# A recurrence that feeds a feed-forward network: a reordered opening before the first dense matmul

## The chip, the cores and the metric

The kernel runs on one core of a Trainium2 chip. The metric is the device time of one execution in microseconds (us), lower is better. A core has five engines with queues of their own: TensorE (PE, with weight loads listed as PEld), VectorE (DVE), ScalarE (ACT), GpSimd (POOL) and SyncE (SP). SP, ACT and POOL also issue the DMA transfers; an issue occupies the queue it stands in. Each engine works through its own list in order, and waits where an instruction needs something of another engine.

## The reference, cut to what matters

All inputs are 32-bit floats.

```python
# q, k, v: (4, 8, 768, 48)   beta: (4, 8, 768)
k_n = k / (norm(k) + 1e-6)
state = zeros(4, 8, 48, 48)
for t in range(768):
    y[:, :, t] = q[:, :, t] @ state
    v_old = state^T k_n[t]
    state = state + beta[t] * outer(k_n[t], v[t] - v_old)
x = y.transpose(0, 2, 1, 3).reshape(3072, 384)
# w1, w2, w3: (384, 768)   w_out: (768, 384)
h = maximum(maximum(x @ w1, x @ w2), x @ w3)
out = h @ w_out                       # (3072, 384)
```

## The kernel before, in words

The 768 steps are cut into 12 chunks of 64 steps. In a chunk, the products of its keys with each other (`gram`, tiles `at`) and of its queries with its keys (tiles `pt`) are made on PE. The chunk's recurrence becomes a triangular system. It is solved once for all batches and heads as blocks of 32 by 32 on DVE (`solve`: for each column one product into `tmp`, L617, and one subtraction from `y_bl`, L621). Two chunks make a pair `m`, and `solve(m)` serves both.

The first pair is different, and it is what the change is about. Its diagonal blocks of 32 are solved only as two halves of 16 (`HB`), so `solve(0)` has 15 columns instead of 31. PE then joins the halves in four matmul steps, each followed by copies out of PSUM: `halves_z` (p_e, L740, into `z`), `halves_u` (p_f, L751, negated back into `ut`), `join_z` (p_z, L768, into `z`) and `join_u` (p_j, L781, negated into `ut`). After these, `ut` holds the chunk's inverse. `new` (p_u, L826) multiplies it with the scaled values, `to_y` (p_y, L868) makes the outputs, and `to_x` (p_x, L887) transposes them into `xt`, the input of the network. For chunk 0 these steps work on two groups of four heads, so that one group's copy runs beside the other's matmuls.

What stands between the solution and `halves_u` is this. `solve(0)` ends with two transposes of 128x512 (L634) that turn the solution `y` back into `x_bl`; `placed` (L557) copies pieces of it into `ut`, on DVE, ACT and POOL; `halves_t` transposes `ut` into the tiles `t` (L700, L702), the stationary side of p_f.

The network (`ffn`) then runs in 6 groups of 512 tokens. `ffn(0)` is a generator of PE units of three matmuls of 256 columns (p_h, L1303). A table of the kernel (`FIRST`, `LINKS`, `CONVERTED` and others) says what is put into the queues after each unit: the rest of the recurrence, the steps of `solve(1)`, and the conversion of weights. In `ffn(0)` the steps of chunk 1 stand between the units: p_e, then p_s (L849, the update of the state, added by DVE at L856), p_f, then p_k (L798, the keys times the new state), and so on.

The weights arrive as 64-bit words in 24 pieces. `fetch` requests a piece into one of 5 buffers `w_bits`; `weights` makes three ACT passes on it (L255, L256, L257), `joined` makes a shift on DVE (L266) and an addition on POOL (L270) that writes `w_sb`. The join of one piece is made when the next is converted (`join_last`).

The order of all queues is written out by hand; no scheduler changes it. The opening is the straight list of calls in L1382 to L1464. Tiles are recycled: PSUM has three buffers of the tag `two`, so the fourth allocation waits for the copy out of the first.

Of the kernel before, what the change touches and what calls it, by code (L numbers as in the profile page):

```python
# [18 lines left out]
BL = 32  # L19
# [4 lines left out]
def kernel(  # L24
# [205 lines left out]
    waiting = []  # L230

    def join_last():
        if waiting:
            joined(*waiting.pop())

    def weights():
# [3 lines left out]
        for n, (dst, _, (a, b)) in enumerate(pieces):  # L240
            if n == 3 * FT:
                join_last()
                yield
            bits = staged.popleft().rearrange("p (a b two) -> p a b two", a=a, two=2)
            low, high = bits[:, :, :, 0], bits[:, :, :, 1]
            mant = work.tile([128, 384], U32, name="mant", bufs=2)
            up = work.tile([128, 384], I32, name="up", bufs=2)
# [7 lines left out]
            nc.scalar.mul(mant_v.bitcast(FP32), high.bitcast(FP32), 2.0**-112)  # L255
            nc.scalar.mul(halves[0], low, 2.0**-29)  # L256
            nc.scalar.mul(halves[1], high.bitcast(FP32), 2.0**-64)  # L257
            join_last()
# [299 lines left out]

    def solve(m):
# [27 lines left out]
        if m < 3:  # L587
            norm(k_bl, nt, root)
# [10 lines left out]
        nc.vector.tensor_tensor(out=xb, in0=xb, in1=by, op=ALU.mult)  # L599
        yield  # L600
# [26 lines left out]
        if m == 0:  # L627
            bl_0.append(k_bl)
            back, ahead = in_rows(xs[0]), y.rearrange("p c i -> p i c")
            A, V, P = nc.scalar.copy, nc.vector.tensor_copy, nc.gpsimd.tensor_copy  # L630
            for part, copies in (
                (slice(HB, BL), (P, A, P, A)), (slice(0, HB), (V, P, V, A)),
            ):
                nc.vector.transpose(out=back[:, part], in_=ahead[:, part])  # L634
                for i, copy in enumerate(copies):
                    placed(0, i, copy, part)
            yield
            return
# [65 lines left out]
    def heads_of(c, name, w):  # L704


        copies = (nc.scalar.copy,) if c else (nc.scalar.copy, nc.vector.tensor_copy)
        n = H // len(copies)
        for i, copy in enumerate(copies):
            p_v = ps_two(name)[:, :, 0 : n * w]  # L710
# [5 lines left out]
    def negated_of(c, name, w):  # L716
        if c:
# [3 lines left out]
        p = [  # L721
            ps_two(name)[:, :, 0 : NP * w].rearrange("p g (h x) -> p g h x", x=w)
            for _ in range(3)
        ]
        yield range(NP), (p[0], p[0]), (nc.scalar.mul,) * 2
        yield range(NP, H), (p[1], p[2]), (nc.scalar.mul, nc.vector.tensor_scalar_mul)
# [4 lines left out]
    def halves_z(c):  # L731
# [4 lines left out]
        for hs, p_v, copy in heads_of(c, "p_e", BL):  # L736
# [24 lines left out]
    def join_z(c):  # L761
        at = [ats.pop(2 * c + g) for g in range(2)]
        z, second = zs[c % NU], ut[c % NU][:, :, :, BL:C]
        for hs, p_v, _ in heads_of(c, "p_z", BL):
            for i, h in enumerate(hs):
                for bb, g in TILES:
                    r = block(bb, 1)
                    nc.tensor.matmul(  # L768
                        p_v[block(bb ^ g), g, i], at[g][r, h, 0:BL], second[r, g, h]
                    )  # L770
            for bb in range(2):
                nc.scalar.copy(z[block(bb), :, span(hs)], p_v[block(bb)])
# [101 lines left out]
    def to_x(c):  # L874
# [8 lines left out]
        for g in range(2):  # L883
# [9 lines left out]
            if not c:  # L893
                nc.scalar.copy(xt[:, g], of[:, g])  # L894
# [489 lines left out]
    load_beta_0()  # L1384
    load_k(6)
    load_q(0)
    load_k(7)
    load_q(1)
    fetch(nc.sync)
    busy(6, ident)  # L1390
# [15 lines left out]
    load_q(2, (nc.gpsimd, nc.gpsimd))  # L1406
    turn(4, (0,))
    turn(5, (0,))
    some(solving, 1)
    keys(4)  # L1410
    keys(5)
    turn(6, (0,))
    turn(0, (1,))
    load_q(3, (nc.gpsimd, nc.gpsimd))
    load_v(0)
    for _ in range(2):
        fetch(nc.sync)
    load_beta()
    keys(6)
    gram(0, (1,), None, later=True)()  # L1420
    turn(7, (0,))
    turn(1, (1,))
    keys(7)
    turn(2, (1,))
    gram(1, (1,), None, later=True)()
    some(conv, 1)
    turn(3, (1,))
    scores = [gram(n, (1,), None, later=True) for n in (2, 3)]
    some(solving, HB + 1)
    for copied in scores:  # L1430
        copied()
    halves_t(0)
    halves_z(0)
    first_norms()
    some(conv, 1)
    placed(1, 0)
# [214 lines left out]
```

## Time and profile before

Three timed executions took 501.72, 502.57 and 502.66 us; the median is 502.57 us. The profiled execution took 501.92 us, of which the span from first to last instruction is 500.0 us, so 1.92 us lie around it.

| | |
|---|---|
| PE busy | 480.2 us (96%) |
| DVE busy | 348.8 us (70%) |
| ACT busy | 169.6 us (34%) |
| POOL busy | 196.1 us (39%) |
| first matmul of the network (p_h) | at 44.06 us |
| chain that ended last | PE 88%, DVE 3%, DMA 2%, ACT 2%, "issue" 2% |
| mean granted TensorE clock | 0.976 |

How to read it: times are counted from the start of the span. A line of the timeline is a run of like instructions: start, length, engine, source line, operation, output and input, shapes, count, and in brackets the idle time before it with what ended it. "issue" is time in which an engine waited for nothing that the profile shows. A table by stretches gives, for each stretch, its length and then the busy time and the number of instructions of PE, PEld, DVE, ACT and POOL, then the granted clock, the share of the DMA engines, and GB/s. A 32-bit matmul stands as two PE and two PEld instructions, a transpose as one and one.

### The profile page before, as it was taken

The page shows a single profiled execution, that of the slowest core. Times are in us where ns is not written, and L with a number is a line of the kernel's source. Part 1 is how long each engine was busy: PE and PEld are TensorE (multiplying, and loading weights), DVE is VectorE, ACT ScalarE, POOL GpSimd, SP SyncE. Part 2 cuts the span into 40 slices and gives each one's busy share as a digit, 9 for nine tenths or more (in the row PEclk, how much of TensorE's full clock was granted, in tenths as well). Part 3 has the DMA queues.
Part 4 walks back from the last instruction along what each step waited for, and adds up shares of the span by engine and source line. Part 5 has one row for each costly group of instructions (what it writes and reads, how often), then busy time and mean ns, then how long its engine had stood idle before and what let it go on. Part 6 is the DMA issues. An engine that isn't in the chain of part 4 may idle for free.

```text
span 500.0 us, 18781 instructions
## 1 busy us (share of the span) xinstructions
PE 480.2 (96%) x8100; PEld 343.4 (69%) x8100; DVE 348.8 (70%) x819; ACT 169.6 (34%) x329; POOL 196.1 (39%) x330
## 2 busy tenths in 40 slices
PE   7869799999999999999999999999999999999997
PEld 6658688878665556565555565565797457988896
DVE  4888898656697352979552998565998864468753
ACT  5686665985330153201243200252211032212310
POOL 6557684764670394780575870601000020000000
PEclk9767899999999999999999999999999999999999
DMA  8948979874351655543775552833223330330001
GB/s 107 168 100 220 211 178 137 199 218 77 81 144 34 140 117 121 138 126 88 155 129 120 146 135 65 176 50 93 65 68 79 61 72 19 86 77 15 1 16 49
DMA packets 110114, 53.51 MB, mean 107 GB/s; under 512 B 93264, under 2 KB 103920, under 8 KB 110032
## 3 DMA queue, kind: packets, MB, share of 16 engines
q1 hardware_dynamic: 98528, 32.01, 31.8%
q0 software_dynamic: 9088, 19.72, 15.8%
q8 instruction: 64, 1.05, 0.9%
q10 hardware_dynamic: 2416, 0.59, 0.7%
q14 instruction: 18, 0.15, 0.1%
HBM read 39.17 MB, written 13.11 MB: 105 GB/s over the span
## 4 chain that ended last, share of the span: by engine, by line
PE 88%; DVE 3%; DMA 2%; ACT 2%; issue 2%; POOL 1%; SPq 1%; DVEq 0%; POOLq 0%; ACTq 0%
PE p_h L1303 34%; PE p_o L1346 13%; PE p_o L1040 10%; PE p_g L443 5%; PE p_c L1241 4%; PE p_u L826 3%; PE p_y L868 3%; PE p_k L798 2%; PE p_m L960 2%; PE p_t L366 2%; PE p_q L798 2%; PE p_s L849 2%; PE p_j L781 2%; PE p_z L768 2%; PE p_e L1241 1%
## 5 line engine op out<-in xcount | busy, mean ns | idle before, releaser
L1303 PE MATMUL p_h<-xt,w_sb 128*128 128x512 f32 (+1 forms) x468 | 177.7, 523 | 0.6 <-ACT xt L894 0.3
L1303 PEld LDWEIGHTS p_h<-xt,w_sb 128*128 128x128 f32 x468 | 85.1, 191 | 62.0 <-issue 53.0
L1317 DVE TENSOR_TENSOR h<-h,p_h 128x512 f32<-128x512 f32 (+1 forms) x42 | 23.9, 569 | 55.9 <-PE p_h L1303 53.4
L617 DVE TENSOR_TENSOR tmp<-x_bl,y_bl 128x31 f32<-128x31 f32 (+20 forms) x139 | 50.3, 362 | 4.0
L621 DVE TENSOR_TENSOR y_bl<-y_bl,tmp 128x31 f32<-128x31 f32 (+20 forms) x139 | 46.5, 334 | 4.8
L1346 PE MATMUL p_o<-wo_sb,h 128*128 128x384 f32 x144 | 49.2, 490 | 0.4 <-POOL wo_sb L270 0.4
L1313 ACT ACTIVATE h<-p_h 128x512 f32<-128x512 f32 (+1 forms) x30 | 16.6, 552 | 76.2 <-PE p_h L1303 76.2
L401 POOL DMA_DIRECT2D turned<-in_q_dram x72 | 39.2, 552 | 5.1 <-POOL turned L396 2.6
L1346 PEld LDWEIGHTS p_o<-wo_sb,h 128*128 128x128 f32 x144 | 26.8, 190 | 18.5 <-POOL wo_sb L270 1.0
L443 PEld LDWEIGHTS p_g<-kqt 48*64 48x64 f32 x1184 | 23.5, 138 | 11.5 <-issue 7.1
L443 PE MATMUL p_g<-kqt 48*64 48x64 f32 (+1 forms) x1184 | 26.7, 238 | 2.9 <-ACT kqt L372 2.9
L270 POOL TENSOR_TENSOR w_sb<-mant,up 128x384 int32<-128x384 int32 x18 | 18.5, 1032 | 23.7 <-DVE mant L266 20.0
L1352 ACT COPY o_sb<-p_o 128x384 f32<-128x384 f32 x12 | 5.7, 478 | 61.7 <-PE p_o L1346 41.7
L396 POOL MEMSET turned<- 128x96 f32 x18 | 3.3, 190 | 59.1 <-DVE kqt L417 59.1
L653 POOL DMA_DIRECT2D ut<-y_d x4 | 2.6, 651 | 60.4 <-DMA y_d<-y_bl 60.4
L148 POOL DMA_DIRECT2D v_t<-in_v_dram x14 | 11.6, 830 | 28.7 <-PE p_u L826 28.7
L856 DVE TENSOR_TENSOR st<-st,p_s 48x768 f32<-48x768 f32 (+1 forms) x18 | 17.1, 951 | 7.7 <-PE p_s L849 7.3
L810 DVE TENSOR_TENSOR v_t<-v_t,p_k 128x768 f32<-128x768 f32 x11 | 10.4, 949 | 15.3 <-PE p_k L798 15.3
L1346 PE MATMUL p_o<-w_sb,xt 128*128 128x384 f32 x60 | 21.0, 486 | 0.0
L427 DVE TENSOR_TENSOR pt<-p_g,mask 128x512 f32<-128x512 f32 x20 | 13.7, 689 | 10.4 <-PE p_g L443 10.3
L460 ACT COPY at<-p_g 128x512 f32<-128x512 f32 x22 | 12.7, 583 | 18.8 <-DVE pt L427 16.5
L401 POOL DMA_DIRECT2D turned<-in_k_dram x32 | 17.5, 553 | 3.0 <-DMA v_t<-in_v_dram 1.9
(252 smaller groups left out, 917.4 us busy)
## 6 DMA issues: line engine op xcount, KB each, us to landing
w_bits<-in_moe_w_dram SPq DMA_DIRECT2D x9, 384.0 KB, 5.3
w_bits<-in_moe_w_dram POOLq DMA_DIRECT2D x9, 384.0 KB, 4.8
turned<-in_q_dram POOLq DMA_DIRECT2D x72, 48.0 KB, 2.6
out_dram<-o_sb SPq DMA_DIRECT2D x34, 96.0 KB, 2.3
y_x<-y SPq DMA_DIRECT2D x32, 96.0 KB, 2.3
qall<-y_x SPq DMA_DIRECT2D x32, 96.0 KB, 2.9
v_t<-in_v_dram POOLq DMA_DIRECT2D x14, 192.0 KB, 4.5
at_d<-at SPq DMA_DIRECT2D x76, 32.0 KB, 2.9
```

The costliest lines, as they stand in the source:

```text
L270: nc.gpsimd.tensor_tensor(out=dst.bitcast(I32), in0=mant_v.bitcast(I32), in1=up_v, op=ALU.add)
L401: (queue, nc.gpsimd)[i].dma_start(out=t[p0 : p0 + 32, bb, at : at + NP * 2 * D].rearrange("p (j x) -> p j x", j=NP), in_=(k, q)[i][2 * bb ...
L443: nc.tensor.matmul(p_g[rows(bb ^ (g * i)), par, c0 : c0 + C * (1 + whole)], kq[:, 0], kq if whole else kq[:, i],)
L617: nc.vector.tensor_tensor(out=t_v, in0=row.to_broadcast(t_v.shape), in1=column.to_broadcast(t_v.shape), op=ALU.mult,)
L621: nc.vector.tensor_tensor(out=rest, in0=rest, in1=t_v, op=ALU.subtract)
L798: nc.tensor.matmul(p_b[rows(bb), par, c0 : c0 + D], kqt[g][dims(par), j, bb ^ g, i], st[dims(par), bb ^ g, g, j],)
L856: nc.vector.tensor_tensor(out=s_v[r], in0=s_v[r], in1=p_s[r, :, 0 : H * D], op=ALU.add)
L1040: nc.tensor.matmul(to[:, g], a[j][:, 128 * g : 128 * (g + 1)], b[j], start=(start and g == of[0] and j == 0), stop=(stop and g == of[-1] a ...
L1241: nc.tensor.matmul(to, w[stays], moves, start=(n == 0), stop=(n == len(terms) - 1))
L1303: nc.tensor.matmul(p_h, w_sb[i][:, t, f * 128 : (f + 1) * 128], xt[:, t, lo : lo + w], start=(t == 0), stop=(t == KT - 1),)
L1317: nc.vector.tensor_tensor(out=h, in0=h, in1=p_h, op=ALU.max)
L1346: nc.tensor.matmul(p_o, stays, moves, start=(n == 0), stop=(n == len(terms) - 1))
```

## The change

All of it lies in the first chunk and in the requests and conversions around it.

- `solve(0)` no longer turns its solution back itself. The opening does it: the second half of the columns first (`turned_back(second)`), then `corners`, a transpose of the solution's first 16 rows straight from `y`, whose pieces `corner` copies into the tiles `t` (zeroed before by POOL) on DVE, POOL and ACT; then the first half. `halves_t(0)` is gone. The early `return` of `solve` for pair 0 is gone too, so its 16th step now also writes the solution to DRAM (two requests of `y_d`, which nothing reads).
- The copies of the score products `pt` of chunk 1 are made before the solve ends, not after.
- The request for q(0) goes to POOL, ahead of its copies; its transpose and product move forward. Two weight pieces and v(0) are requested ahead of the writes of `at`.
- The requests of `blocks(1)`, of v(1) and of three weight pieces move from POOL to SP, and so do two of the requests in `ffn(0)`.
- `weights` now hands back control after each ACT pass. The first two pieces are converted before the solve ends, the third in single passes between the copies of chunk 0; the joins are made later, and the third piece uses spare room in `wo_sb`.
- `AHEAD` names 14 products of the identity with itself, which nothing reads, put in front of the first head group of p_e (6), p_f (1), p_z (2), p_j (2), p_u (1) and p_y (2).
- For chunk 0, p_z multiplies whole 64x64 tiles, so that one copy of 128 partitions takes the place of two of 32; both p_e and p_z groups are copied by ACT; both negations of the second group of p_f go to DVE; the second half of `xt` is copied by DVE.
- The four copies `placed(1, ...)` of chunk 1 and the masks of chunk 0 are spread differently among the steps.

```diff
     def join_last():
         if waiting:
-            joined(*waiting.pop())
+            joined(*waiting.popleft())
...
             nc.scalar.mul(mant_v.bitcast(FP32), high.bitcast(FP32), 2.0**-112)
+            yield
             nc.scalar.mul(halves[0], low, 2.0**-29)
+            yield
             nc.scalar.mul(halves[1], high.bitcast(FP32), 2.0**-64)
-            join_last()
+            if len(waiting) > held[0]:
+                join_last()
...
+    def turned_back(part):
+        nc.vector.transpose(
+            out=in_rows(xs[0])[:, part],
+            in_=solved[0].rearrange("p c i -> p i c")[:, part],
+        )
+
+    def corners():
+        by_column = t1[1].rearrange("p g h x -> p (g h x)").rearrange(
+            "p (c x) -> p c x", x=BL
+        )
+        nc.vector.transpose(out=by_column, in_=solved[0][:, 0:HB])
+        return by_column
+
+    def corner(by_column, i, g, copy):
+        bb, half = divmod(i, 2)
+        copy(
+            fine[0][g][block(bb ^ g, half), :, BL * half : BL * half + HB],
+            by_column[block(bb, half), :, H * g : H * (g + 1)].rearrange(
+                "p c h -> p h c"
+            ),
+        )
...
-        if m == 0:
-            bl_0.append(k_bl)
...
-            for part, copies in (
-                (slice(HB, BL), (P, A, P, A)), (slice(0, HB), (V, P, V, A)),
-            ):
-                nc.vector.transpose(out=back[:, part], in_=ahead[:, part])
-                for i, copy in enumerate(copies):
-                    placed(0, i, copy, part)
-            yield
-            return
...
+    def warmed(p, n):
+        for _ in range(n):
+            nc.tensor.matmul(p[:, 0, 0:128], ident, ident)
+        return p
+
+    AHEAD = dict(p_e=(6, 0), p_f=(1, 0), p_z=(2, 0), p_j=(2, 0), p_u=(1, 0), p_y=(2, 0))
...
+                    if c < 2 * FINE:
+                        nc.tensor.matmul(
+                            p_v[rows(bb ^ g), g, i],
+                            at[g][rows(bb), h],
+                            second[rows(bb), g, h],
+                        )
+                        continue
...
+            if c < 2 * FINE:
+                copy(z[:, :, span(hs)], p_v)
+                continue
...
     load_beta_0()
+    load_q(0, (nc.gpsimd, nc.gpsimd))
     load_k(6)
-    load_q(0)
-    load_k(7)
     load_q(1)
     fetch(nc.sync)
+    load_k(7)
...
+    fetch(nc.sync)
+    fetch(nc.sync)
+    blocks(1)
+    load_v(1)
+    fetch(nc.sync)
+    some(solving, HB)
+    first, second = slice(0, HB), slice(HB, BL)
+    turned_back(second)
+    of_first = corners()
+    for i, copy in enumerate((P.tensor_copy, A.copy, P.tensor_copy, A.copy)):
+        placed(0, i, copy, second)
+    for i in range(4):
+        for g, engine in enumerate((V if i < 3 else A, P if i < 3 else A)):
+            corner(of_first, i, g, engine.copy if engine is A else engine.tensor_copy)
+    turned_back(first)
     halves_z(0)
     first_norms()
...
-    blocks(1, nc.gpsimd)
-    for _ in range(2):
-        fetch(nc.gpsimd)
     halves_u(0)
     turn_t1(0)
     join_z(0)
+    join_last()
+    masked(pts[0], by_par(pts[0]))
+    some(conv, 1)
     join_u(0)
+    masked(pts[1], by_par(pts[1]))
+    some(conv, 1)
     old_k(0)
     old_q(0)
     new(0)
+    join_last()
+    placed(1, 0)
+    placed(1, 1, nc.gpsimd.tensor_copy)
     some(conv, 1)
-    fetch(nc.gpsimd)
-    load_v(1, nc.gpsimd)
+    to_y(0)
+    join_last()
+    placed(1, 2)
+    busy(2, ident)
+    to_x(0)
+    busy(1, ident)
     placed(1, 3)
```

## The prediction

> **What bounds the kernel now.** I read the slices of the page first, then the timeline of the opening, then tables by stretches.
>
> ```profile
> span 500.0 us, 18781 instructions
> PE   7869799999999999999999999999999999999997
> PEclk9767899999999999999999999999999999999999
> q8 instruction: 64, 1.05, 0.9%
> ```
>
> From the fifth slice (50 us) on, PE is at 9 tenths nearly everywhere: what the opening gains should stay to the end. Before that PE waits, and its clock is cut. In the timeline the opening is a chain in which PE is short and copies and transposes lie between:
>
> ```profile
> 25.24 2.03 DVE L634 STREAM_TRANSPOSE x_bl<-y_bl 128x512 f32<-128x512 f32 x2
> 29.18 0.71 DVE L700 STREAM_TRANSPOSE t<-ut 128x512 f32<-128x512 f32 x1 [0.55 <-ACT pt L454]
> 29.92 1.44 DVE L702 STREAM_TRANSPOSE t<-ut 64x512 f32<-64x512 f32 x2
> 31.39 0.42 DVE L743 COPY z<-p_e 128x256 f32<-128x256 f32 x1
> 32.56 1.73 ACT L755 ACTIVATE ut<-p_f 16x128 f32<-16x128 f32 x6 [1.30 <-PE p_f L751]
> 34.89 1.52 ACT L772 COPY z<-p_z 32x256 f32<-32x256 f32 x4 [0.61 <-PE p_z L768]
> 37.30 2.18 PE L826 MATMUL p_u<-v_t,ut 64*64 64x48 f32 x64 [0.19 <-issue]
> 39.26 2.00 PE L868 MATMUL p_y<-u,pt 64*64 64x48 f32 x64
> 44.06 2.86 PE L1303 MATMUL p_h<-xt,w_sb 128*128 128x256 f32 x12 [0.34 <-ACT xt L894]
> 50.97 0.94 DVE L856 TENSOR_TENSOR st<-st,p_s 128x768 f32<-128x768 f32 x1
> 55.37 0.37 PE L798 MATMUL p_k<-st,kqt 48*64 48x48 f32 x9 [2.38 <-issue]
> ```
>
> The solve ends at 25.21. Until 31.4 DVE makes t, until 34.0 the negations run, y is complete at 41.89 (L872), and the network starts at 44.06. The last line matters as much: 55 of 64 records of p_k had run, then PE stood for 2.38 us with "issue" named. The stretches say what that is:
>
> ```profile
> 29.50:32.90 3.40, 2.47 (x74) 2.10 (x67) 3.18 (x7) 2.05 (x6) 0.42 (x1) 0.50 0.23 38
> 36.30:39.75 3.45, 3.18 (x119) 2.86 (x118) 2.27 (x5) 2.29 (x7) 2.02 (x3) 0.50 0.62 195
> 39.75:43.20 3.45, 3.45 (x65) 3.36 (x58) 3.03 (x7) 2.37 (x6) 2.29 (x3) 0.51 0.55 192
> 46.11:49.20 3.09, 2.82 (x130) 2.34 (x128) 2.88 (x11) 1.99 (x4) 2.55 (x4) 1.00 0.87 195
> 49.20:55.30 6.10, 3.74 (x127) 3.12 (x127) 4.83 (x13) 3.30 (x8) 5.24 (x5) 1.00 1.11 223
> ```
>
> The last two stretches end where PE stood with "issue" (49.25 and 55.37); each holds about 256 PE and PEld instructions. The queue named instruction moved 64 packets of 16.4 KB, which is 256 instructions of 64 bytes. So PE's program comes in blocks of 256, and PE stands if the next is late. The packet for the stand at 49.25 began at 46.42, that for 55.37 at 52.54: 2.83 us each. The previous block began at 46.11 and 49.25, so the request needed another 0.3 and 3.3 us. The first three stretches show the clock: half from 29.5 to 43.2.
>
> **Part 1, up to the solve's end: nothing.** q(0) leaves SP (two requests, 1.31 us) for POOL (two, 1.41 us), which is idle from 5.7 to 8.18. SP now has eleven requests between beta and the first at write instead of nine, about 0.65 each, so that write leaves 1.3 later, or more where SP waits for a piece to land; its result is wanted only by solve(1). k(7), moved behind q(1) and a piece, is wanted later than before. Two zeroings on POOL (0.98 for 1056 columns, so about 0.5 each) stand after the diagonal's copy, which solve needs. q(3) behind them still leaves about 0.9 earlier, as the five norm operations (1.6) now follow it; the norms are wanted at 29. ACT gets the three passes of a second piece (1.47 together) and both pt copies (1.07); it idled 3.8 us between 14 and 26. So ACT is free at about 26.3. If q(0)'s copy made ACT late at 14.3, solve would slip by up to 0.6.
>
> **Part 2, solve's end to p_z.** DVE: 1.01 for one half of L634, 0.71 for the corners (contiguous like L700), three corner copies. No row has their shape; bounds are 0.19 (the smallest DVE operations of 32 columns) and 0.66 (a 32x256 copy of L557 beside POOL); I take 0.33, half of it, as they have half its elements. So t is done on DVE at 28.0. POOL does two L557 copies (0.67 each, to 27.7) and three corners at about 0.35: 28.8. ACT: L557 twice (0.65, to 27.7), two corners to 28.4, two z copies (0.39) to 29.4, as p_e starts at 27.75. So p_f runs at 28.95 instead of 31.42, and negations end at 31.4 (four of 0.31 on DVE) instead of 34.0: 2.6 earlier.
>
> **Part 3, to y.** p_z on whole tiles costs what p_e does (0.69 for 32 records at full clock, against 1.08 for 64 of p_z at half), and its two copies of 0.39 replace four of 0.38; t1 takes 1.35 on DVE as before and is ready at 32.8, so p_j ends 33.9, its negations 34.4. One identity product before p_u stands on the path, since its PSUM buffer is freed by those negations: about 0.24 (a third of p_h's 1.30 is 0.43 for 256 columns, so 0.22 for 128; L1377 shows 0.39 for one with its tail). The two before p_y cost 0.45, as PE has just finished p_u. The others lie in waits. At full clock (64 records of p_y at 67.86: 1.15) p_u and p_y end at 35.6 and 37.15; with a shift (0.35) and placed(1,0) (0.6) ahead of DVE's copy, y is complete at 37.8, 4.1 earlier.
>
> **Two prices on top.** First, blocks: counted in the changed program's order, block borders fall in the middle of p_e, early in p_z, on p_u's first product and at the end of p_y; before, the last fell in p_h. A request seems to leave some 64 instructions past a border (28.25 to 29.55, 34.44 to 35.30), so border to border costs at least 0.55+0.35+2.83 = 3.7. The chain wants 3.2, 3.2 and 2.55, so PE stands 0.5, 0.5 and 1.2: 2.2. Bounds: 0 (if blocks come earlier than I infer) and 2.2 plus three times 2.1, the request's extra under load at 38.16 to 40.85. Second, the clock: if it falls at 29.5 as before, p_u and p_y cost about 1.0 each more (2.18 and 2.00 against 1.1), which swallows the third stand; then it is 2.2-1.2+2.0 = 3.0. I take the middle, 2.6: y at 40.4.
>
> The clock's row first: 2.17 busy of 3.40 (26.1 to 29.5) was followed by half clock, 3.45 of 3.45 by full. [...]
>
> **Part 4, y to p_k.** What ends last there is DVE. Before, from y (41.89) to the end of the state's addition (51.91) DVE was busy for 10.02 without a gap, and p_k began at 51.96. Now placed(1,2) (0.60), half of xt (0.56, nearest row L872) and placed(1,3) (0.60) lie in it too: 11.8. p_k begins at 52.2, no earlier than before. But the block that was late there is requested earlier: its border, 4.2 after p_h starts (42.0), is at 46.2; 1.3+2.1+2.83 later is 52.4, before p_k's 56th record at 53.1. So PE goes on at 53.1 instead of 55.37: 2.3 less. Requests moved to SP free POOL of 4.6 us of issue, hidden work. On SP the moved requests lie where it idled (31 to 45.5); blocks(1) lands near 36, wanted at 39. The two y_d writes (0.5 MB) load the DMA engines only; their cost is in the blocks' bounds. A piece that waits on SP for ACT's third conversion holds q(4) behind it, to about 41; before, q(4) left at 46.1. The weight joins on POOL end before their p_h.
>
> **Sum.** Against the profiled execution (500.0 and 1.92 around, 501.92) 2.3 less is 499.6. That execution lies 0.65 under the median; carried to the median, 502.57-2.3 = 500.3.
>
> **Rivals.**
> A: blocks hardly cost. y at 37.8, p_k at 49.6, its 56th record at 50.5: 4.9 less, 497.7. For it: before, only 0.28 was lost to blocks between 28 and 44. Against: intervals there were 6.2, 3.7 and 8. [...]
> B: no change in effect: DVE's longer list after y and the blocks eat all, 502.6 within 1.0.
> C: slower. The moved requests (512 KB, 2x192 KB, three pieces of 384 KB, 512 KB of y_d) load the DMA engines just from 28 to 38, where they were nearly idle (38 GB/s from 29.5 to 32.9). Each of three blocks then leaves 2.1 later: y at 46.7, p_k at 58.5 and its 56th record at 59.4, 4.0 later, 506.6. It decides once the three extras together pass 2.3, and counts as slower from 3.3. For it: 3.3 at 49.25 under 223 GB/s. Against: 0.3 at 46.11 under similar load.
>
> **How the numbers follow.** No change is within 0.2%, 1.0 us, about what a measurement here can tell. Forecast 0.50 (gain 1.1 to 3.6 by y between 39.1 and 41.6: 499.0 to 501.5), A 0.18, B 0.13, C 0.19. Faster 0.68, same 0.13, slower 0.19. The range takes in A and C's nearer half: 497.2 to 503.6.
>
> **What would show it.** Right: the corner copies done near 28.8, p_f near 29, PE stands with "issue" in p_z, p_u and p_y, p_h near 42, p_k near 52, no stand inside p_k. Wrong: the clock stays full and no stands occur (A), or stands of over 1.5 us each (C), or solve's end moves, or a weight join comes last before p_h.

## The result, and the profile after

The changed kernel is slower. Its median is 507.0 us (19 executions, 504.91 to 510.3); the kernel before, run beside it, has 502.75 us (19 executions). The ratio is 1.009, with a 95% interval of 1.0069 to 1.0111, so about 4.3 us are lost. The forecast was 500.3 us. The profiled execution took 509.68 us and is 2.7 us above its median; executions of one kernel lie 2 to 9 us apart here. Below, times are judged by medians and ratios, and profiles are used for places.

The page of the changed kernel, span, PE and its granted clock in 40 slices, and the queue named instruction, whose 64 packets fit PE's 16256 PE and PEld instructions at 254 each:

```profile
span 507.9 us, 18851 instructions
PE   7697889998999999999999999999999999999996
PEclk9787989999999999999999999999999999999999
q8 instruction: 64, 1.05, 0.9%
```

After the opening the page looks like that of before. The timeline shows where the time went:

```profile
20.08 1.09 PE L376 MATMUL p_t<-ident,kmore 128*128 128x128 f32 x4 [2.88 <-DMA kmore<-in_k_dram]
26.63 1.33 DVE L587 COPY t<-t 32x128 f32<-32x128 f32 x3
27.83 2.69 PE L732 MATMUL p_e<-ident 128*128 128x128 f32 x12
29.61 1.27 ACT L567 COPY ut<-x_bl 32x256 f32<-32x256 f32 x2
32.49 1.14 PE L788 MATMUL p_f<-z,t 64*64 64x32 f32 x64
37.80 0.49 PE L732 MATMUL p_u<-ident 128*128 128x128 f32 x2 [0.59 <-ACT ut L831]
40.64 1.96 PE L874 MATMUL p_u<-v_t,ut 64*64 64x48 f32 x64 [2.36 <-issue]
42.53 1.22 PE L732 MATMUL p_y<-ident 128*128 128x128 f32 x4
48.60 2.83 PE L1351 MATMUL p_h<-xt,w_sb 128*128 128x256 f32 x12 [0.52 <-DVE xt L942]
57.87 1.15 PE L846 MATMUL p_k<-st,kqt 48*64 48x48 f32 x64 [1.87 <-DVE st L904]
69.96 1.03 PE L874 MATMUL p_u<-v_t,ut 64*64 64x48 f32 x56 [1.63 <-issue]
71.71 2.77 PE L1351 MATMUL p_h<-xt,w_sb 128*128 128x256 f32 x6
126.28 0.33 PE L453 MATMUL p_g<-kqt 48*64 48x64 f32 x2 [1.90 <-issue]
```

The line numbers are those of the changed kernel: p_f is L788 (L751 before), p_u L874 (L826), p_h L1351 (L1303). Two rows of the kernel before belong beside the last three: the p_h behind the second chunk's p_u, and the p_g that has no stand there:

```profile
66.47 1.46 PE L1303 MATMUL p_h<-xt,w_sb 128*128 128x256 f32 x6
118.06 0.69 PE L443 MATMUL p_g<-kqt 48*64 48x64 f32 x32
```

Read against before, mark by mark, in the two profiled executions:

| PE starts | before | after | later by |
|---|---|---|---|
| p_f (bulk) | 31.42 | 32.49 | 1.1 |
| p_u | 37.30 | 40.64 | 3.3 |
| p_h, the network | 44.06 | 48.60 | 4.5 |
| p_k, with the new state | 51.96 | 57.87 | 5.9 |
| p_z of chunk 1 | 57.44 | 60.44 | 3.0 |
| next chunk's p_k | 76.32 | 82.69 | 6.4 |
| p_k at 120 | 120.17 | 128.03 | 7.9 |

The chain's data reach p_u 0.9 later. Then PE stands 2.36 with "issue" before p_u. The stand of 2.38 inside p_k is gone, as forecast (5.9 falls to 3.0). But 3.4 are lost again between 60 and 76, where PE stands 1.63 in p_u and the p_h behind it takes 2.77 instead of 1.46, at half clock, and 1.5 more up to 126, where another stand of 1.90 is. Neither of the two is in the forecast's sum. From there to the end it stays 7.4 to 8.6 behind.

### The profile page after: what moved, and what is told of

It reads as the page before. It is cut to its first block, busy times and chain, and to the rows that moved or that the text cites. A ratio compares the mean times of both kernels' runs of the same rounds, so it can differ in the third digit from the quotient of the medians.

```text
span 507.9 us, 18851 instructions
## 1 busy us (share of the span) xinstructions
PE 484.3 (95%) x8128; PEld 347.4 (68%) x8128; DVE 348.1 (69%) x821; ACT 168.9 (33%) x326; POOL 194.4 (38%) x330
## 3 DMA queue, kind: packets, MB, share of 16 engines
q8 instruction: 64, 1.05, 0.9%
## 4 chain that ended last, share of the span: by engine, by line
PE 87%; DVE 5%; issue 3%; DMA 2%; ACT 1%; POOL 1%; SPq 0%; DVEq 0%; POOLq 0%; ACTq 0%
PE p_h L1351 32%; PE p_o L1394 13%; PE p_o L1088 12%; PE p_c L1289 5%; PE p_g L453 4%; PE p_y L916 3%; PE p_u L874 3%; PE p_m L1008 2%; PE p_k L846 2%; PE p_q L846 2%; PE p_t L376 2%; PE p_j L829 2%; PE p_s L897 1%; DMA qall<-in_q_dram 1%; PE p_z L813 1%
## 5 line engine op out<-in xcount | busy, mean ns | idle before, releaser
L1351 PE MATMUL p_h<-xt,w_sb 128*128 128x512 f32 (+1 forms) x468 | 177.8, 524 | 1.7 <-issue 0.9
L1351 PEld LDWEIGHTS p_h<-xt,w_sb 128*128 128x128 f32 x468 | 85.3, 191 | 63.1 <-issue 54.2
L659 DVE TENSOR_TENSOR y_bl<-y_bl,tmp 128x31 f32<-128x31 f32 (+20 forms) x139 | 50.2, 361 | 4.8
L655 DVE TENSOR_TENSOR tmp<-x_bl,y_bl 128x31 f32<-128x31 f32 (+20 forms) x139 | 47.1, 339 | 4.0
L280 POOL TENSOR_TENSOR w_sb<-mant,up 128x384 int32<-128x384 int32 x17 | 17.4, 1029 | 29.3 <-DVE mant L276 20.9
L148 POOL DMA_DIRECT2D v_t<-in_v_dram x12 | 9.9, 830 | 29.3 <-PE p_u L874 29.3
L874 PEld LDWEIGHTS p_u<-v_t,ut 64*64 64x64 f32 x768 | 13.5, 142 | 10.2 <-issue 8.8
L470 ACT COPY at<-p_g 128x512 f32<-128x512 f32 x22 | 12.7, 584 | 19.0 <-DVE pt L437 17.3
```

Of the source, the lines that this page charges most:

```text
L280: nc.gpsimd.tensor_tensor(out=dst.bitcast(I32), in0=mant_v.bitcast(I32), in1=up_v, op=ALU.add)
L655: nc.vector.tensor_tensor(out=t_v, in0=row.to_broadcast(t_v.shape), in1=column.to_broadcast(t_v.shape), op=ALU.mult,)
L659: nc.vector.tensor_tensor(out=rest, in0=rest, in1=t_v, op=ALU.subtract)
L874: nc.tensor.matmul(p_v[rows(bb ^ g), g, i], ut[c % NU][rows(bb), g, h], rhs[rows(bb), g, h],)
L1351: nc.tensor.matmul(p_h, w_sb[i][:, t, f * 128 : (f + 1) * 128], xt[:, t, lo : lo + w], start=(t == 0), stop=(t == KT - 1),)
```

## Experiments

Each ratio is to the kernel before, run in the same series, from 4 to 12 executions of the edited kernel; the intervals are 95%. Theories, named in the expectations: R, requests put ahead make k(7) and q(3) late; A, ACT's list is too long; P, the identity products cost PE time; B, the moved requests delay PE's program blocks; S, the added products shift every block border behind them.

### The early requests, the products and the unread writes, one at a time

k(7) ahead again:

```diff
-    load_q(1)
-    fetch(nc.sync)
     load_k(7)
+    load_q(1)
+    fetch(nc.sync)
```

> The changed kernel with one request put back: k(7) leaves SP ahead of q(1) and the first weight piece, as before the change; all else stays. Theory R (requests): k(7) and q(3) come late behind the requests put ahead of them, PE stands 2.88 us before k(7)'s transposes, its clock falls, ACT gets through its list 3 us later than before. By R this one request gives back part of it: it leaves about 2.0 earlier, the stand falls from 2.88 to under 1, PEclk in 20 to 25 us is above 0.5, ACT's two L567 copies start at 27 to 28.5 instead of 29.61, and the time is 1 to 3 us under that of the changed kernel (507.0). Theory B (blocks): the loss is PE's stand of 2.36 before p_u, whose program block came late under the transfers of 34.75 to 40; that stays and the time is within 1 us of 507.0. Theory P (identity products): within 1 us of 507.0.

Measured: 507.44, ratio 1.0113 (1.0083 to 1.0143). The stand for k(7) is gone, but q(3) then ended a wait of 4.06 at 24.88, ACT's copies and p_e came no sooner (30.67), and the time is that of the changed kernel.

All early requests in the old order: the same edit, and

```diff
-    for _ in range(2):
-        fetch(nc.sync)
-    load_v(0)
     turn(4, (0,))
...
     load_q(3, (nc.gpsimd, nc.gpsimd))
+    load_v(0)
+    for _ in range(2):
+        fetch(nc.sync)
```

> The changed kernel with all early requests back in their old order: k(7) ahead of q(1) and the first piece; two weight pieces and v(0) behind q(3) instead of ahead of it. Theory R: q(3) then lands in 4 to 5 us instead of 7.14, k(7) by 17.5, PE has no stand over 1.5 us between 16 and 26, ACT's L567 copies start by 27.0, p_e near 27.8, p_f near 29.5 to 30, and the time is 3 to 5 us under the changed kernel: 502 to 504, about the time before. Theory B: the stand before p_u stays over 2 us and at most 1 us is won, 506 to 507. Theory P: no change.

Measured: 507.92, ratio 1.0126 (1.0071 to 1.0181). p_e came at 29.68, 0.8 earlier, and p_u's data 0.8 earlier, but the stand before p_u grew:

```profile
40.97 1.96 PE L874 MATMUL p_u<-v_t,ut 64*64 64x48 f32 x64 [3.45 <-issue]
```

R describes what PE and ACT do before 30, but not where the time is lost: what the chain gains, the block takes.

Without the identity products:

```diff
-    AHEAD = dict(p_e=(6, 0), p_f=(1, 0), p_z=(2, 0), p_j=(2, 0), p_u=(1, 0), p_y=(2, 0))
+    AHEAD = dict(p_e=(0, 0), p_f=(0, 0), p_z=(0, 0), p_j=(0, 0), p_u=(0, 0), p_y=(0, 0))
```

> The changed kernel without the identity products in the waits of p_e, p_f, p_z, p_j, p_u and p_y (they write nothing that is read). Theory P: the six before p_e ran at half clock from 27.83 to 30.52 and ended as p_e's data came; those before p_u and p_y lie on the path: 0.3 to 0.5 and 1.1 at half clock, so the time falls by 1 to 1.7 us, to 505.5. Theory B: 14 products are 56 PE instructions less, so each border between program blocks moves by up to 56 instructions; the stand before p_u moves to another place, and the time is within 1 us of 507.0. Theory R: within 1 us of 507.0.

Measured: 506.07, ratio 1.0089 (1.0058 to 1.0120); no gain that can be told. PE stood at other places, first in p_g, then 1.55 in p_z, 0.61 and 0.99 in p_u:

```profile
24.47 1.11 PE L453 MATMUL p_g<-kqt 48*64 48x64 f32 x27 [2.52 <-issue]
```

In this one execution the granted clock also came to full only at 17.3 us (5.6 before), and the solve ended at 27.8.

Without the writes of `y_d`:

```diff
-    some(solving, HB)
+    some(solving, HB - 1)
```

> The changed kernel without the two writes of y_d for the first group (0.5 MB that nothing reads; solve(0) is stopped one step earlier). Theory B: these writes leave SP at 39.50, after the late block's packet at 38, so the stand before p_u stays; the blocks at 43 and 49.8 may come earlier; 0 to 1 us less. The fetches behind them leave 1.2 earlier. Theory R and P: within 0.5 us of the changed kernel, 506.5 to 507.5.

Measured: 509.53, ratio 1.0141 (1.0089 to 1.0193). No cost of the writes shows; p_u stood 2.63 without them.

### What delays a block

The chain's requests back on POOL, behind the first weight join, and no writes of `y_d`:

```diff
-    fetch(nc.sync)
-    fetch(nc.sync)
-    blocks(1)
-    load_v(1)
-    fetch(nc.sync)
-    some(solving, HB)
+    some(solving, HB - 1)
...
     masked(pts[0], by_par(pts[0]))
+    blocks(1, nc.gpsimd)
+    load_v(1, nc.gpsimd)
+    for _ in range(3):
+        fetch(nc.gpsimd)
```

> The changed kernel with blocks(1), v(1) and the three weight pieces behind them back on POOL's queue, after the first weight join (POOL is there at 38.3 us), and without the unread y_d writes. SP then issues nothing between the at writes (31.5) and the network. Theory B (blocks): the program block for p_u was late (packet at 38.0, some 2 us after its request) because these transfers filled 34.75 to 40 with 240 GB/s; without them the packet starts by 36.5, the stand of 2.36 before p_u falls under 0.8, p_u starts at 38.2 to 38.9 instead of 40.64 and p_h at 46 to 47 instead of 48.60, unless a later block is late in turn; time 504 to 506. Theory A (ACT's list: the second piece's passes and half clock up to 29 make ACT 3 us late) and theory R (early requests): no change, 506 to 508.

Measured: 506.21, just above the range of B, ratio 1.0081 (1.0038 to 1.0124). The stand before p_u is gone:

```profile
39.08 1.96 PE L874 MATMUL p_u<-v_t,ut 64*64 64x48 f32 x64 [0.16 <-POOL w_sb L280]
47.10 2.83 PE L1351 MATMUL p_h<-xt,w_sb 128*128 128x256 f32 x12 [0.58 <-DVE xt L942]
```

The reverse, on the kernel before: its chain requests moved to SP, nothing else.

```diff
+    blocks(1)
+    for _ in range(3):
+        fetch(nc.sync)
+    load_v(1)
     halves_t(0)
...
-    blocks(1, nc.gpsimd)
-    for _ in range(2):
-        fetch(nc.gpsimd)
...
-    fetch(nc.gpsimd)
-    load_v(1, nc.gpsimd)
```

> The kernel before, with nothing changed but the requests of blocks(1), v(1) and three pieces moved from POOL to SP, right behind the at writes, as the change has them. PE's program and its block borders are those of before. Theory B: the packets of the blocks that started at 29.5, 35.25 and 40.7 come 1 to 3 us later, stands with issue of 1.5 to 3.5 us in sum appear between p_z and p_h, the network starts at 45.5 to 47.5 instead of 44.06; time 503.5 to 506. Theories A, R and P: the transfers are hidden and POOL loses 4.6 us of issue work, so within 1 us of before.

Measured: 504.77, ratio 1.0038 (0.9999 to 1.0076). The stand appears in p_u, with PE's program as it was:

```profile
37.19 0.89 PE L826 MATMUL p_u<-v_t,ut 64*64 64x48 f32 x23 [0.19 <-issue]
41.47 1.32 PE L826 MATMUL p_u<-v_t,ut 64*64 64x48 f32 x41 [3.40 <-issue]
47.58 2.86 PE L1303 MATMUL p_h<-xt,w_sb 128*128 128x256 f32 x12 [0.33 <-ACT xt L894]
```

The mechanism can be timed. The block border in question lies in p_z. In each kernel the stretch from PE's passing it to the first packet of the next block is the following (columns: stretch, length, busy time and instructions of PE, PEld, DVE, ACT, POOL, clock, DMA share, GB/s). The kernel before:

```profile
34.55:35.30 0.75, 0.66 (x51) 0.52 (x39) 0.72 (x2) 0.38 (x2) 0.69 (x2) 0.50 0.00 0
```

The same kernel with the requests on SP:

```profile
34.45:38.55 4.10, 3.19 (x137) 2.52 (x127) 3.45 (x6) 2.57 (x7) 1.57 (x2) 0.50 0.92 293
```

The changed kernel:

```profile
34.50:38.00 3.50, 2.84 (x132) 2.45 (x130) 3.28 (x9) 2.29 (x6) 0.69 (x1) 1.00 0.78 242
```

The changed kernel with the requests on POOL:

```profile
35.15:36.40 1.25, 1.25 (x65) 1.21 (x61) 1.16 (x4) 0.37 (x1) 0.00 (x0) 1.00 0.00 0
```

In these four profiles the packet follows 0.75 and 1.25 us after the border with idle DMA engines, 3.5 and 4.1 with 242 and 293 GB/s. From the packet to PE's going on it is 2.6 and 2.9 in the two that stood. So B is shown in place and size by the traces of this border; the time of the moved requests alone, 0.38%, has an interval that just reaches no change. The rate alone does not set the delay: in the kernel before, a packet came 1.4 after the border at 61.48 under 268 GB/s. By these rows (an estimate) a border would pay nothing where its 256 instructions last longer than delay and fetch together, 6.1 and 7.0 us here; no run tests that limit.

The second piece's ACT passes out of the way:

```diff
         copied()
-        some(conv, 3 * (n == 2))
...
     halves_z(0)
+    some(conv, 1)
...
     halves_u(0)
+    some(conv, 1)
...
     masked(pts[1], by_par(pts[1]))
-    some(conv, 1)
+    some(conv, 2)
```

> The changed kernel with the second weight piece's three passes on ACT moved from between the pt copies (27.60 to 29.1) into ACT's waits in the chain (one behind z of p_e, one behind the negations of p_f, one behind z of p_z; the third piece's follow one place later). Theory A: ACT's L567 copies start at about 28.1 instead of 29.61, p_e at 29.0 to 29.5 instead of 30.45, and the data of p_u are ready at 37.0 instead of 38.2; time 505 to 506.5. Theory B: p_u waits for its block, which was requested when PE passed the border before; that moves by as much as the chain, but the transfers that delay it do not, so the stand grows instead: p_u at 40 to 40.6 and less than 0.7 won.

Measured: 509.69, ratio 1.0162 (1.0110 to 1.0213). ACT's copies came at 28.34, but the six products held PE from 27.60 to 30.52 and p_e started at 30.44, as before this edit; p_u stood 2.42. So A alone is not the cause.

All three put back, by the edits shown above together (early requests, chain requests, passes); the products are kept:

> The changed kernel with all three put back: early requests in the old order, the requests of the chain on POOL and no y_d, the second piece's passes in ACT's waits. The new transposes, whole-tile p_z and identity products stay. If R, A and B together are the loss, then the forecast of the prediction holds here: p_e at 27.7 to 28.5, p_f at 29.5, p_u at 36 to 37.5 with a stand under 1, p_h at 43 to 45.5, p_k at 52.5 to 54.5, time 499.5 to 503. If the loss lies in the transposes or in the products themselves (theory P), the time stays at 505 to 508.

Measured: 507.66, ratio 1.0126 (1.0069 to 1.0183). The opening did what was expected up to p_u (37.07, no stand; p_k 54.50), and yet nothing was won. The profile shows the loss far behind the change:

```profile
117.81 1.03 PE L1351 MATMUL p_h<-xt,w_sb 128*128 128x256 f32 x4
118.77 0.69 PE L453 MATMUL p_g<-kqt 48*64 48x64 f32 x30
121.63 0.47 PE L453 MATMUL p_g<-kqt 48*64 48x64 f32 x2 [2.18 <-issue]
122.04 2.50 PE L1351 MATMUL p_h<-xt,w_sb 128*128 128x256 f32 x5
```

and the clock behind it, in stretches of 3.4 us:

```profile
118.80:122.20 3.40, 1.22 (x34) 0.97 (x33) 0.99 (x5) 1.54 (x3) 0.99 (x1) 0.85 0.28 43
122.20:125.60 3.40, 3.40 (x34) 2.39 (x35) 0.90 (x2) 0.38 (x1) 0.99 (x1) 0.50 0.02 5
125.60:129.00 3.40, 3.40 (x113) 3.30 (x110) 1.33 (x3) 0.00 (x0) 0.71 (x1) 0.50 0.02 5
129.00:132.40 3.40, 3.40 (x74) 2.40 (x76) 0.42 (x1) 0.00 (x0) 1.71 (x7) 0.64 0.00 0
```

Between 110 and 126 us this execution fell from 1.4 to 7.7 behind before: 2.2 by the stand, the rest because PE then ran at half clock for some 10 us (121.2 to 131.4) though it was busy almost without a gap. The clock fell after a stretch that was not idle, with 1.66 busy of 3.40 (117.80 to 121.20; the stretches above do not begin where the clock changes), and came back only after three more, with 2.97, 3.40 and 3.40 busy.

### Where the borders fall

That a stand with "issue" is a block border can be counted. Put PE's instructions in the order of their start (PE, PEld and the waits on PE's queue): of the 96 such stands of over 0.3 us in the 20 profiles of this case, 90 come at number 193 or 194 of a block of 256, whatever the kernel.

The 14 products are 28 PE and 28 PEld instructions (PE x8128 against x8100 without them), so every border behind them lies some 53 to 56 instructions earlier in the work. The kernel of the last run without its products:

```diff
-    AHEAD = dict(p_e=(6, 0), p_f=(1, 0), p_z=(2, 0), p_j=(2, 0), p_u=(1, 0), p_y=(2, 0))
+    AHEAD = dict(p_e=(0, 0), p_f=(0, 0), p_z=(0, 0), p_j=(0, 0), p_u=(0, 0), p_y=(0, 0))
```

> The changed kernel with early requests in the old order, the chain's requests on POOL, no y_d, the second piece's passes in ACT's waits (the run before had these three), and now also without the identity products. Theory P: at half clock the six before p_e ran from 26.60 to 29.35 in that run while p_e's data were there at 28.6, the one before p_u took 0.79 and the two before p_y 1.15: without them the network starts 1 to 1.7 us earlier, at 43.4 to 44.1 instead of 45.14. Theory S (borders shifted): the products also moved every later block border 56 instructions; without them the borders of the network lie within 3 instructions of those of the kernel before, so the stand of 2.18 at 121.6 and the half clock behind it (in sum 6 us between 110 and 126 us) do not occur, and the time is 499 to 502. If P holds and S does not: 505 to 506.5.

Measured: 503.55, ratio 1.0011 (0.9986 to 1.0035), against 1.0126 with the products, and as fast as before. The network started at 44.85 against 45.14, so the products' own time is only 0.3 of that in these two profiles; behind 76 us this execution is at most 1.3 behind before, and nothing stands near 121. The time lies above the 499 to 502 of S, but the kernel before had 503.2 in this series against the 502.1 that the forecast started from. S fits, P alone does not.

The borders alone, on that kernel:

```diff
     busy(6, ident)
+    p_pad = ps_ffn([128, TOK], "p_w")[0:32, 0:32]
+    for _ in range(13):
+        nc.tensor.matmul(p_pad, ident[0:32, 0:32], ident[0:32, 0:32])
```

> The same kernel with 13 more products of 32x32 in the warming at the start (52 instructions, 0.3 us, in a wait for k): nothing else changes but where the block borders fall, some 52 instructions earlier in all the work behind, as in the changed kernel. Theory S: stands with issue in other places than without them, in the opening or near 121 us, and the time differs by 1.5 to 6 us from the run without the 13 products. Without S: within 0.7 us of it.

Measured: 508.38, ratio 1.0101 (1.0077 to 1.0124), 4.8 more. It is not a clean measure: in the profile the 13 products took 1.59 us (the 0.3 expected was the author's estimate), PE stayed at half clock behind them, and the solve ended 2.2 later. So up to 2.2 of the 4.8 need not be the borders.

The same 13 products on the kernel before:

> The kernel before with 13 products of 32x32 more in the warming at the start (52 instructions, 0.3 us in a wait for k), and nothing else: all block borders behind fall 52 instructions earlier in the work, within one instruction of where the changed kernel has them in the network. Theory S: the borders' places alone cost a large part of what the change lost, so this is 1.5 to 5 us slower than before. Rival W (it is the work that the change moved, not the borders): within 0.7 us of before.

Measured: 507.16, ratio 1.0067 (1.0038 to 1.0097), 3.4 us. Here the 13 products took 1.12 us and the solve ended only 0.4 later (25.62), so in this profile at most 0.4 is theirs. The timeline of this kernel:

```profile
38.04 0.26 PE L781 MATMUL p_j<-z,t 32*32 32x32 f32 x2 [0.52 <-issue]
44.26 0.45 PE L868 MATMUL p_y<-u,pt 64*64 64x48 f32 x3 [2.18 <-issue]
58.99 0.78 PE L798 MATMUL p_k<-st,kqt 48*64 48x48 f32 x35 [2.48 <-issue]
108.47 0.38 PE L768 MATMUL p_z<-ut,at 32*32 32x32 f32 x20 [0.94 <-issue]
```

Before, PE came to the border that is now in p_y's last records only in p_h, at 46.11, 5.3 after the block's first packet (40.85); here it came at 42.08, 0.35 after the packet (41.73), and stood. The stand of 2.48 in p_k has one of 2.38 as its counterpart before. Of the 5.0 that this execution is longer than the profile of before, 3.65 are there when the network starts (47.71 against 44.06), most of it in the first two stands. Nothing of the change is in this kernel, so S is shown: the places of the borders alone move the time. One rival was not run by itself: the 13 products also take one PSUM buffer more, so that the two buffers of their tag change places in all later work.

The traces bear S out behind the opening too. Nine of the profiles have the borders shifted by the 14 or the 13 products, and each has a stand of 0.46 to 2.18 in p_z at 108 to 111 us or in p_g at 121 to 127. Of the other eleven two have one over 0.4 there: 0.91 at 119.60 with the requests on SP, and 0.59 at 123.07 in the first of the two runs that follow.

The reverse: the borders put back by 57 small products in place of the six of the warming (51 more, 204 instructions), on the changed kernel, and on the one that has the three put back and keeps its products:

```diff
-    busy(6, ident)
+    p_pad = ps_ffn([128, TOK], "p_w")[0:32, 0:32]
+    for _ in range(57):
+        nc.tensor.matmul(p_pad, ident[0:32, 0:32], ident[0:32, 0:32])
```

> The changed kernel with the six warming products at the start replaced by 57 of 32x32 (204 instructions more, about 3.1 us instead of 2.93 in the same wait): the borders of all work behind fall within one instruction of where the kernel before has them, and all requests, products and copies stay as changed. Theory S: no stand at 126 us and fewer behind 57; the stand in the opening stays somewhere, since the requests that delay the blocks stay (theory B): 503.5 to 506. Rival W: 506 to 508.

Measured: 510.69, ratio 1.0141 (1.0097 to 1.0185).

> The kernel with early requests, chain requests and passes put back, with the identity products kept (1.0126 of before), and the same 57 small products at the start, so that the borders fall where before has them. It tells the products' own cost from the shift that they make. Theory S: no stand and half clock at 121 to 131 us, 502.5 to 504.5, within 1 us of the kernel without products. Theory P (the products themselves cost 4 us): 506.5 to 508.5.

Measured: 506.44, ratio 1.0078 (1.0034 to 1.0121), against 1.0126 unaligned; the two intervals overlap. Both were spoilt: the solve ended at 28.88 and 30.00, 4 and 5 us late, behind a padding that ended 3.4 later than the warming did and a clock that came to full at 11.6 and 14.2 instead of 5.6. The first settles nothing. The second has no stand near 121, as S had it, but one of 2.75 in p_s, and its time lies outside the range of S and at the edge of that of P. That its solve is 5 us late and its ratio no worse is in favour of S, no more.

### Are the two causes enough?

The changed kernel with the chain's requests on POOL and without products; early requests and passes stay as changed:

> The changed kernel with only the two causes taken out that the runs so far show: the chain's requests back on POOL behind the first weight join (and no y_d), and no identity products, so that the borders lie within 3 instructions of before. The early requests (two pieces and v(0) ahead, k(7) behind a piece) and the second piece's passes between the pt copies stay as changed. If the two causes suffice: 502 to 505, within 1 us of the kernel before. If the early requests (theory R) cost on their own, because they load the DMA engines from 14 to 25 while blocks are fetched there: a stand in p_g near 24 as in the run without products (2.52 at 24.47), the end of the solve at 26.5 to 28 instead of 25, and 505 to 507.

Measured: 504.71, ratio 1.0018 (0.9989 to 1.0047). So the kernel without the two causes is as fast as before, within the interval, with the early requests and the passes as changed:

| | with products | without |
|---|---|---|
| chain's requests on SP | 1.0090 (the change) | 1.0089 |
| on POOL | 1.0081 | 1.0018 |

Taking out one of them gives next to nothing, both give 0.7%. On the kernel before the two alone cost 0.67% and 0.38%, which adds up to 1.05%, against the 0.90% measured for the change; no run has both on the kernel before. Why one alone does not show on the changed kernel was not settled. The two profiles suggest that late blocks found other places (with requests on SP and no products 1.55, 0.61 and 0.99 in p_z and p_u; with requests on POOL and products 1.99 in p_u at 68.93), but they are one execution each.

### A faster version?

If load delays blocks, requests that are not yet wanted should wait. On the kernel before:

```diff
-        if i == 1:
-            load_q(4)
-            load_q(5)
-        if i == 2:
-            load_q(6)
+        if i in (3, 4, 5):
+            load_q(i + 1)
```

> The kernel before with one thing changed: the requests of q(4), q(5), q(6) (six of 96 KB) leave with the third, fourth and fifth product step of the network instead of the first and second; they are first wanted at 65.97, 70.30 and 72.76. Theory B: the block behind the stand of 2.38 at 55.37 was 3.6 us from its border to its packet because the DMA engines moved 200 to 250 GB/s from 48 to 52; with 0.4 MB less there the packet comes by 51, the stand falls under 1 and the time by 1 to 2.4 us, to 499.5 to 501. Otherwise: within 0.7 of the kernel before (502.1).

Measured: 502.03, ratio 0.9975 (0.9948 to 1.0001). The stand of 2.38 in p_k became 1.04, but p_u and p_s behind it now stood 0.74 and 1.30, where before they stood 0.22 and 0.21. Once more:

> The kernel before with q(4), q(5), q(6) requested later, once more (0.9975, interval 0.9948 to 1.0001 in the run before). If the gain is real: a ratio of 0.995 to 0.999 again, with no stand over 1.3 us at p_k. If it was chance: 0.999 to 1.003.

Measured: 503.96, ratio 0.9992 (0.9958 to 1.0026); p_k stood 1.04 again. If there is a gain, it is 0.2%, and these runs do not show it for sure. With v(2) later too:

```diff
-        if i in (3, 9, 10, 21):
-            load_v((3, 9, 10, 21).index(i) + 2)
+        if i in (6, 9, 10, 21):
+            load_v((6, 9, 10, 21).index(i) + 2)
```

> The kernel before with q(4), q(5), q(6) requested later, as in the run before (0.9975), and v(2) too (two of 192 KB, at the sixth product step instead of the third). Theory B: with less to move from 52 to 58 us the stands of 1.04 at 53.16 and 0.74 at 63.88 shrink: 0.5 to 1.5 us under that run, 499.5 to 501.5. Otherwise within 0.5 us of it.

Measured: 504.24, ratio 1.0013 (0.9980 to 1.0046): nothing. And the kernel with the three put back and no products, with q(4) to q(6) later:

> The kernel of the first run of this call with q(4), q(5), q(6) requested later in the same way. If the two gains add: the network starts at 43.4 to 44.1, p_k runs without a stand by 53.5, and the time is 497 to 500.5, under both kernels. If p_k waits for the state's addition on DVE all the same, this run is as long as the one without the later requests.

Measured: 504.33, ratio 1.0020 (0.9996 to 1.0044). No version here is shown to beat the kernel before. This last profile also shows the forecast's chain under its best conditions, without late requests and without a stand before p_u:

```profile
27.89 0.43 PE L777 MATMUL p_e<-ut,at 64*64 64x32 f32 x4 [1.40 <-POOL ut L567]
28.57 1.81 PE L777 MATMUL p_e<-ut,at 64*64 64x32 f32 x58 [0.26 <-POOL t L587]
30.23 1.97 PE L788 MATMUL p_f<-z,t 64*64 64x32 f32 x62
33.11 2.17 PE L806 MATMUL p_z<-ut,at 64*64 64x32 f32 x64 [0.92 <-POOL v_t L334]
36.98 1.96 PE L874 MATMUL p_u<-v_t,ut 64*64 64x48 f32 x64 [0.52 <-POOL w_sb L280]
```

p_e comes when forecast (27.75), but from 24 to 41 the clock is at half, each step takes about twice what was put down for it, and p_u starts at 36.98 instead of 37.30: of the 2.6 us forecast for the transposes, 0.3 reach p_u.

## Why the prediction was wrong, step by step

The miss is 6.7 us (507.0 against 500.3), and but for 0.2 by which the median before came out higher it has two parts. One is the forecast gain of 2.3, which no version here shows: without the moved requests and the products the kernel measures 1.0011 and 1.0018 of before. The other is the loss of 4.3. The first part is answered under Part 2, the second here.

**"What the opening gains should stay to the end."** This is the step that failed. The sum stops at p_k (53.1 against 55.37): it counts the block borders up to there and has no term for those behind. But the products lengthen PE's program, all borders behind them move, and the stands behind 57 us (1.63 and 1.90 in the profile after, with half clock behind the first) are new. They take that execution from 3.0 behind before to 7.9. The shift alone, on the kernel before, measured 3.4 us, in that kernel for the most part before the network. And the opening gained nothing that could have stayed: the network started 4.5 later in the profile after.

**The two prices.** The blocks' term was 2.2 in the sum, 2.6 with the clock, with three extras of 2.1 as its upper bound, which made rival C. One of the three borders in the opening paid such an extra, the one in p_z: 3.5 to its packet instead of 0.75, and 2.36 of stand before p_u. C was right in mechanism and sign, and the moved requests alone measured 1.9 us (0.38% of 502, an interval that just reaches none); the sum had them as a bound, not as a term. C missed that the larger part of the loss, by the two runs on the kernel before, needs no load from these requests. The row that spoke against C, 0.3 at 46.11 under 194 GB/s, was one fetch. At four borders whose 256 instructions lasted 3.6 to 4.1 us the profiles show stands of 2.18 (p_y, the 13 products), 2.36 (p_u, the changed kernel), 2.38 (p_k, the kernel before) and 3.40 (p_u, the requests on SP).

**Part 1, "nothing".** Right for the solve's end (24.8 against 25.2). Wrong in "k(7) is wanted later than before": its landing ended a PE wait of 2.88. Wrong in "q(3) still leaves about 0.9 earlier" as to its landing: behind two pieces and v(0) it took 7.14 us against 4.1 to 4.7, and its transposes came at 24.89 instead of 23.84. So ACT was free for its copies at 29.6, not 26.3. It did not decide: putting the requests back changed no time.

**Part 2.** The corner copies were put at 0.33 and measured 0.44, within the bounds of 0.19 to 0.66. This term failed as well: the 2.6 us gained up to p_z's data were not there, negations ended at 35.0 instead of 31.4. In the changed kernel ACT was late; with that put right, products at half clock held PE up to p_e's start; without the products, p_e, p_f and p_z themselves ran at half clock, where the sum had them at full clock. The clock was priced only from p_u on. And where the borders lie as before, the block that was late in p_k is late in p_s: the kernel of 1.0011 stood 2.27 there and 0.56 in p_k, against 0.32 and 2.38 before.

**Part 3.** The product before p_u was put at 0.24 and took 0.49, those before p_y 0.45 and took 1.22, the first at full clock, the others at half. With the products the clock was full from 30.1 to 40.4 in the changed kernel; without them it was half from 19.8 to 43.7 in the one of 1.0011, and from 33.65 to 37.10 in the changed kernel. But the six before p_e took 2.69 at half clock, and in the two pairs of profiles that differ in the products alone and have no long stand before p_h, the network starts 0.3 and 1.1 later with them (45.14 and 44.85, 47.10 and 46.03). The rest of what they cost, they cost through the borders.

**Part 4.** Right: DVE's longer list ends last before p_k (1.87 of waiting for the state's addition), and p_k runs without the stand of 2.38. From p_h to p_k it is 9.3 instead of 7.9; the forecast had 10.2. Its p_h at 42.0 lies 1.6 behind y at 40.4; the rows have 2.2 before and 2.1 after, so by its own terms it is 42.5.

**The rivals.** A needed blocks that cost nothing, B that they eat just the gain. C was on the right side with 506.6 against 507.0 measured, by an arithmetic (three extras of 2.1 in the opening) that the profile does not bear out, so that its number is near by luck. Its chance of 0.19 was too low: the trace had a stand of 2.38 at one of 64 borders, the change moves nearly all of them, and the sum priced the three of the opening and the one in p_k.

## What to carry to other kernels

An instruction added to a PE-bound program that streams in blocks does not act in its own place alone (here 13 products cost 0.67%, and PE stood 2.18 us in p_y): count how many instructions it shifts the rest by, and look where the borders behind it then fall. A transfer that is hidden from every engine's waits can still delay the program's own fetches (here 4.10 us from border to packet instead of 0.75, and a stand of 3.40); look at which of the program's blocks is fetched meanwhile. Before trusting a gain of a few us in an opening, shift the kernel before by a few idle instructions: if that alone moves the time as much, gains of that size belong to the alignment, not to the change.

## What was not expected of the hardware

- 52 unread PE instructions at the start, 1.1 us of work mostly in a wait, made a 502 us kernel 0.67% slower: most of it 33 to 39 us later, a part at places over 100 us later.
- The time from a border to the next block's first packet was, at the border in p_z, 0.75 and 1.25 us with the DMA engines idle and 3.5 and 4.1 us with 242 and 293 GB/s moving, in the four profiles shown. It is not the rate alone: 1.4 us under 268 GB/s occurs too.
- A stand of 2.18 us at 119 us cost some 6 us, since the clock was at half for about 10 us of nearly gapless work behind it.
- 13 products of 32x32 took 1.12 us in one kernel and 1.59 in another, at the same place in the same wait, and in the second the half clock that followed made the solve end 2.2 later. The clock came to full at 5.2 us in the first and at 10.5 in the second; over all 20 profiles that moment lies between 4.9 and 17.3 us, also for kernels that start alike.
